# Sparse attention feeding a token mixer: the values of a pair of query blocks in two halves, by batch

## The chip, the cores and the metric

The kernel runs on one core of one Trainium2 chip. The metric is the device time of one execution in microseconds (us), lower is better. TensorE is PE in the profile, VectorE is DVE, ScalarE is ACT, GpSimd is POOL and SyncE, which issues most DMAs, is SP.

## The reference, cut to what matters

Four batches, eight heads, 768 positions in 24 blocks of 32, head size 64. Every query block attends to the first and the last block, to its neighbours and to three sampled blocks; the first and the last query block attend to all. The result goes through a mixing layer.

```python
scores = scale * np.matmul(q, k.transpose(0, 1, 3, 2))
mask = np.abs(blk_i - blk_j) <= window            # window = 1, blocks of 32
mask = mask | (blk_i == 0) | (blk_j == 0) | (blk_i == n_blocks - 1) | (blk_j == n_blocks - 1)
for qb in range(n_blocks):
    for kb in sampled_blocks[qb]:
        mask[qb * block:(qb + 1) * block, kb * block:(kb + 1) * block] = True
attn = softmax(np.where(mask, scores, -1e9))
x = np.matmul(attn, v)                            # heads side by side: [4, 768, 512]
theta = x @ w_theta
y = w_tok_r @ (x * cos(theta)) + w_tok_i @ (x * sin(theta))     # over positions, by batch
u = x + y
out = u + np.maximum(u @ w_ch, 0.0)
```

## The kernel before

The program has two parts, `attention` (until about 265 us) and `token_mix` (the rest). Attention goes through the batches in two passes of two batches each, `bp` 0 and 1; in the code below `b` is the batch within the pass. A pass is a row of **units**: four wide units for the first and the last query block (names with `w`), then 22 narrow units, one for each query block `i` from 1 to 22. Two neighbouring narrow units, `i` odd and `i + 1`, make a **pair**, and what the program does from one odd unit to the next is called a **step** here. The order of all instructions is written out by hand (`tc.manual_schedule()`); each engine runs its own list in order.

A narrow block goes through these stages, with the names of their tiles:

- `gather_k` (POOL): copies the block's keys into `kg`: five copies for an odd block, four for an even one. `gather_v` (POOL): an indirect DMA that fetches the block's value rows into one of four buffers `vb`. `load_pair` (SP): a plain load of the values that the two blocks of a pair share, into `va`.
- `scores` (PE): sixteen matmuls into PSUM tile `S` (two buffers); then two reductions on DVE to `m` (the row minima).
- `weights` (ACT): four exponentials from `S` to `P`.
- `turn` (PE, ACT): eight transposes of `P` into the PSUM tile `T`, of which there is one, two banks wide; a copy on ACT from `T` to `pT`. `pT` holds both blocks of a pair, and there is one `pT`.
- `values` (PE): for a whole pair, into the PSUM tile `X` (one, a bank for each batch): for each batch one matmul that zeroes the bank, sixteen small matmuls with `vb` and eight with `va`; here for both batches at once.
- `finish` (DVE, SP): three DVE instructions (`sm`, `sm`, `xo`) and four stores of `xo` to the scratch `xs` in DRAM.

Between these, `Decoder` turns the 64-bit weights of the mixer into float32 pieces: `load` (SP, 512 KB), `start` (ACT, an Abs), `bits` (DVE, three instructions), `rest` (two), `high` (ACT, a cast), `low` (two), in which the next but one piece is loaded. `decoder.ahead(phases)` puts the ACT part at the head of a unit, `decoder.go(phases)` the DVE part behind the weights.

In the step of before, an odd unit `i` has on PE: scores of `i + 1`, values of the pair `i - 2`, transposes of `i`. The even unit behind it has scores of `i + 2` and transposes of `i + 1`. On ACT the odd unit has weights before the copy, the even unit the copy before the weights; so two copies stand behind each other, with at most a decoder instruction between.

Both parts overlap at the end of attention: `follow` is the generator of `token_mix`, and its pieces (`theta`, whose products are the PSUM tiles `h`, and then ACT's `t`, the first reader of `h`) are put between the last units by `next(follow)`.

Of the kernel before, what the change touches and what calls it, by code (L numbers as in the profile page):

```python
# [10 lines left out]
F32 = mybir.dt.float32  # L11
# [9 lines left out]
P = 128  # L21
# [165 lines left out]
def attention(tc, qT, qE, kT, vr, sampled, xs, ident, pieces, room, follow):  # L187
# [8 lines left out]
    nc = tc.nc  # L196
    with ExitStack() as ctx, ExitStack() as scored, ExitStack() as early:
# [10 lines left out]
        ps_t = ctx.enter_context(tc.tile_pool(name="ps_t", bufs=1, space=PSUM))  # L208
# [6 lines left out]
        none = first[0:1, 1:2].bitcast(BF16)[:, 0:1]  # L215
# [7 lines left out]
        kbs, qbs, qes, vws, st, xws, numbers = {}, {}, {}, {}, {}, {}, {}  # L223
# [97 lines left out]
        def turned(pts, out, name):  # L321

            t = ps_t.tile([P, 8, 128], F32, tag="T", name=f"T{name}")
            for k, pt in enumerate(pts):
                nc.tensor.transpose(t[:, k, :], pt, ident)  # L325
            t = t[:, 0 : len(pts)]
            nc.scalar.copy(out, t.rearrange("r k (p q) -> r k p q", p=4) if len(out.shape) == 4 else t)  # L327

        pT_pair = pT.rearrange("r (k p u q) -> r k p u q", k=8, p=4, u=2)
        pT_wide = pT.rearrange("r (e k f) -> r e k f", e=2, k=8)  # L330

        def turn(bp, i):
            s = st[bp, i]
            pts = [s["P"][:, e, b, 128 * c : 128 * c + 128] for c in range(2) for e in range(2) for b in range(2)]
            turned(pts, pT_pair[:, :, :, (i - 1) % 2, :], f"{bp}_{i}")

        def normalised(name, x, n):
            sm = wp.tile([P, 8], F32, tag="sm", name=f"sm{name}", bufs=2)[:, 0:n]
# [8 lines left out]
        def sums_tile(name):  # L347
            return ps_x.tile([P, 2, 512], F32, tag="X", name=f"X{name}")[:, :, 0:260].rearrange("r b (g f) -> r b g f", f=65)

        def values(bp, i):
            x = st[bp, i]["X"] = sums_tile(f"{bp}_{i}")
            va = vas[((i - 1) // 2) % VA_BUFS]
            def weigh(b, e, p, k, u0, n, v, start, stop):
                c, pp = p // 2, p % 2
                r0 = 64 * c + 32 * u0
                v0 = 65 * (8 * b + 4 * pp + 2 * e + c)
                nc.tensor.matmul(  # L359
                    x[r0 : r0 + 32 * n, b, 2 * pp + e, :], pT_pair[:, 4 * k + 2 * e + b, p, u0 : u0 + n, :], v[:, v0 : v0 + 65],  # L360
                    start=start, stop=stop,
                )

            heads = [(b, e, p) for b in range(2) for e in range(2) for p in range(4)]
            for b in range(2):
                nc.tensor.matmul(x[:, b], none.to_broadcast([1, P]), none.unsqueeze(2).to_broadcast([1, 4, 65]), start=True, stop=False)
            for b, e, p in heads:
                for u in range(2):
                    weigh(b, e, p, 1, u, 1, vbs[(i - 1 + u) % VB_BUFS], False, False)
            for b, e, p in heads:  # L370
                weigh(b, e, p, 0, 0, 2, va, False, e == 1 and p % 2 == 1)

        def finish(bp, i):
            xo = normalised(f"{bp}_{i}", st.pop((bp, i))["X"], 8)
            for c in range(2):
                for u in range(2):
                    r0 = 64 * c + 32 * u
                    nc.sync.dma_start(xs[bp][i + u, c].rearrange("q b p f -> q (b p f)"), xo[r0 : r0 + 32])
# [64 lines left out]
        units = []  # L443
# [8 lines left out]
        def do(n, inner, wide=None):  # L452

            if 0 <= n < len(units):
                bp, i, x = units[n]
                if i != "w":
                    inner(bp, i)
                elif wide:
                    wide(bp, *x)

        def is_wide(n):
            return 0 <= n < len(units) and units[n][1] == "w"
# [6 lines left out]
        with tc.manual_schedule():  # L469
            load_edges(0)  # L470
            load_k(0, 0, 2)
            tab = Tables(nc, wp, sampled)
            turn_edges(0)
            load_k(0, 2, 2)
            load_v_wide(0, 0, 0)
            load_k(0, 4, 2)
            load_v_wide(0, 0, 1)
            load_k(0, 6, 2)
            load_v_wide(0, 1, 0)
            load_v_wide(0, 1, 1)  # L480
            for i in (1, 3):
                load_q(0, i)
            decoder = Decoder(pieces, stage, nc.sync)
            do(0, scores, scores_wide)
            tab.make(nc, cp)
            do(0, weights, weights_wide)
            for n in range(len(units) + 1):
                phases = 0
                if n < len(units):
                    phases = round(shares[n] / total * 3 * len(pieces)) - decoder.at  # L490
                if n + 5 < len(units) and not is_wide(n + 5) and units[n + 5][:2] not in ((0, 1), (0, 3)):
                    load_q(*units[n + 5][:2])
                if first_of_pair(n + 10):
                    load_edges(1)
                if first_of_pair(n + 12):
                    load_v_wide(1, 0, 0)
                if first_of_pair(n + 2):
                    for b, pp in WIDE[1:]:
                        load_v_wide(1, b, pp)
                do(n + 2, gather_k)  # L500
                if n == len(units) - 5:
                    follow.send(qp)
                elif n == len(units) - 3:
                    next(follow)
                if 5 <= n < 21 and n % 2:
                    load_k(1, (n - 5) // 2, 1)
                do(n + 3, number_blocks)
                do(n + 2, scale_q)
                if first_of_pair(n + 2):
                    turn_edges(1)  # L510
                decoder.ahead(phases)
                last = None
                if is_wide(n):
                    bp, _, x = units[n]
                    if n and not is_wide(n - 1):
                        last = units[n - 2][:2]
                        values(*last)
                    turn_wide(bp, *x, 0)
                    do(n + 1, scores, scores_wide)
                    if n and is_wide(n - 1):  # L520
                        values_wide(bp, *units[n - 1][2], 1)
                    if is_wide(n + 1):
                        nx = units[n + 1]
                        weights_wide(nx[0], *nx[2], (0,))
                        turn_wide(bp, *x, 1)
                        weights_wide(nx[0], *nx[2], (1,))
                    else:
                        do(n + 1, weights, weights_wide)
                        turn_wide(bp, *x, 1)
                    if last:  # L530
                        finish(*last)
                    decoder.go(phases)
                    if n == 0:
                        tab.rest(nc)
                    values_wide(bp, *x, 0)
                    if n and is_wide(n - 1):
                        finish_wide(bp, *units[n - 1][2])
                elif n == len(units):
                    last = units[n - 2][:2]
                    values(*last)  # L540
                    next(follow)
                    finish(*last)
                else:
                    bp, i, _ = units[n]
                    do(n + 1, scores, scores_wide)
                    if i == 1:
                        values_wide(bp, *units[n - 1][2], 1)
                    elif i % 2:
                        last = bp, i - 2
                        values(*last)  # L550
                    if n == len(units) - 1:
                        scored.close()
                        next(follow)
                    if i % 2:
                        do(n + 1, weights, weights_wide)
                        turn(bp, i)
                    else:
                        turn(bp, i)
                        do(n + 1, weights, weights_wide)
                    decoder.go(phases)  # L560
                    if last:
                        finish(*last)
                    if n >= len(units) - 2:
                        if n == len(units) - 2:
                            early.close()
                        next(follow)
                    if i == 1:
                        finish_wide(bp, *units[n - 1][2])
                do(n + 2, load_pair)
                do(n + 2, gather_v)  # L570
            assert not decoder.left(), decoder.left()


# [298 lines left out]
```

## Time and profile before

| | us |
|---|---|
| three runs | 607.76, 609.36, 615.38 |
| median | 609.36 |
| the profiled execution | 603.66 |
| its span | 601.9 |

The profiled execution is 5.70 us under the median of the runs. Its page has PE busy for 545.9 us (91% of the span), DVE 444.2 (74%), ACT 346.1 (58%) and POOL 150.3 (25%). The granted clock of PE is 0.971 in the mean. In the profile's answers a row has a start, a duration, the engine, the source line, the operation, the tiles written and read, a count, and in brackets the idle time ahead of it with what ended it; "issue" is an end for which the profile shows no cause. A matmul on float32 data of which the program has one stands as two in the counts (S, X).

### The profile page before, as it was taken

Reading aid. Unit: us, or ns where it says so; the run is one execution under the profiler, and the core shown is the slowest. Engines: PE = TensorE matmul, PEld = TensorE weight load, DVE = VectorE, ACT = ScalarE, POOL = GpSimd, SP = SyncE. Lnnn points to the kernel's source line nnn. Section 1 sums busy time; section 2 is a strip of 40 time slices with the busy share of each in tenths; the row PEclk is TensorE's granted clock in tenths of the full one; section 3 lists DMA queues with packets and bytes.
Section 4 is the critical chain, followed back from the end, with each engine's and each line's share of the span. In section 5 each row is a group of like instructions: output and inputs, shape, how many; then the busy total and the mean of one; then the engine's idle time right before and its main releaser. Section 6 shows DMA issues by size and latency. Waiting matters only on the chain.

```text
span 601.9 us, 16838 instructions
## 1 busy us (share of the span) xinstructions
PE 545.9 (91%) x6636; PEld 481.1 (80%) x6636; DVE 444.2 (74%) x1041; ACT 346.1 (58%) x730; POOL 150.3 (25%) x262
## 2 busy tenths in 40 slices
PE   4878787897798988489999999999999999999997
PEld 2556555565565666479999999999999999999997
DVE  3799768878998998598974985757857649548454
ACT  2667757866688787755664743455634456424520
POOL 1459758640578795000000000000000000000000
PEclk9989979998999999959999999999999999999999
DMA  8879999995689899455221241211431111221002
GB/s 296 325 219 313 330 277 354 305 316 174 204 252 285 286 319 256 141 158 143 86 71 35 75 145 57 75 43 50 119 107 62 61 49 32 77 69 60 16 1 105
DMA packets 63263, 95.60 MB, mean 159 GB/s; under 512 B 9168, under 2 KB 44624, under 8 KB 63184
## 3 DMA queue, kind: packets, MB, share of 16 engines
q1 hardware_dynamic: 56848, 71.09, 38.6%
q0 software_dynamic: 6336, 23.43, 11.5%
q8 instruction: 52, 0.85, 0.6%
q14 instruction: 27, 0.22, 0.1%
HBM read 81.90 MB, written 12.58 MB: 157 GB/s over the span
## 4 chain that ended last, share of the span: by engine, by line
PE 76%; DVE 9%; ACT 7%; issue 4%; DMA 3%; SPq 1%; ACTq 0%; DVEq 0%
PE y L676 11%; PE y L677 11%; PE y L678 11%; PE T L325 6%; PE X L359 6%; PE S L307 4%; PE o L701 4%; PE o L700 4%; PE o L699 4%; PE h L638 4%; PE h L640 4%; PE h L639 4%; ACT pT L327 3%; ACT P L319 2%; DMA raw_tok_r<-in_w_tok_r_dram 2%
## 5 line engine op out<-in xcount | busy, mean ns | idle before, releaser
L319 ACT ACTIVATE P<-S,m 128x256 f32<-128x256 f32 x176 | 69.3, 485 | 15.4 <-DVE m L310 12.2
L642 ACT ACTIVATE t<-h,up_int 128x256 f32<-128x256 f32 x48 | 22.8, 475 | 74.5 <-PE h L640 74.2
L310 DVE TENSOR_REDUCE m<-S 128x2 f32<-128x512 f32 x88 | 56.3, 681 | 12.4 <-PE S L307 12.4
L307 PE MATMUL S<-kg,q 64*32 64x256 f32 x1408 | 54.9, 402 | 8.3 <-issue 8.3
L638 PE MATMUL h<-w_theta_hi,xTh 128*128 128x256 f32 x192 | 55.8, 291 | 6.9 <-ACT xTh L629 6.8
L327 ACT COPY pT<-T 128x1024 f32<-128x1024 f32 x44 | 44.8, 1019 | 30.0 <-PE T L325 29.7
L325 PE MATMUL T<-ident,P 128*128 128x128 f32 x352 | 49.1, 283 | 14.0 <-ACT pT L327 11.4
L325 PEld LDWEIGHTS T<-ident,P 128*128 128x128 f32 x352 | 38.4, 143 | 27.3 <-ACT pT L327 21.3
L268 POOL COPY kg<-kb 128x256 f32 (+2 forms) x101 | 53.0, 565 | 19.8 <-PE S L307 19.7
L640 PE MATMUL h<-w_theta_hi,xTl 128*128 128x256 f32 x192 | 55.5, 289 | 1.6 <-DVE xTl L630 1.6
L268 POOL COPY kg<-kb_tok_i 128x256 f32 (+2 forms) x101 | 50.8, 542 | 24.2 <-DVE sb_scratch L175 14.8
L639 PE MATMUL h<-w_theta_lo,xTh 128*128 128x256 f32 x192 | 55.2, 287 | 0.0
L290 POOL DMA_INDIRECT vb<-in_vr_dram,rows x44 | 44.5, 1012 | 39.6 <-PE X L359 33.5
L645 DVE SCALAR_TENSOR_TENSOR rr<-t,h 128x256 f32<-128x256 f32 x48 | 19.8, 414 | 34.6 <-ACT t L643 34.1
L649 ACT ACTIVATE cs<-rr 128x256 f32<-128x256 f32 x48 | 20.0, 416 | 43.5 <-DVE rr L647 43.5
L638 PEld LDWEIGHTS h<-w_theta_hi,xTh 128*128 128x128 f32 x192 | 37.4, 195 | 7.9 <-ACT xTh L629 7.9
L677 PE MATMUL y<-w_tok_r,zh 128*128 128x384 f32 x128 | 43.1, 337 | 0.0
L677 PE MATMUL y<-w_tok_i,zh 128*128 128x384 f32 x128 | 43.1, 337 | 0.0
L678 PE MATMUL y<-w_tok_i,zl 128*128 128x384 f32 x128 | 43.1, 337 | 0.0
L676 PE MATMUL y<-w_tok_i,zh 128*128 128x384 f32 x128 | 43.1, 337 | 0.0
L678 PE MATMUL y<-w_tok_r,zl 128*128 128x384 f32 x128 | 43.1, 337 | 0.0
L676 PE MATMUL y<-w_tok_r,zh 128*128 128x384 f32 x128 | 43.1, 336 | 0.0
(154 smaller groups left out, 1467.7 us busy)
## 6 DMA issues: line engine op xcount, KB each, us to landing
xa<-xs SPq DMA_DIRECT2D x192, 64.0 KB
xr<-xs SPq DMA_DIRECT2D x96, 64.0 KB
out_dram<-of SPq DMA_DIRECT2D x32, 192.0 KB
va<-in_vr_dram SPq DMA_DIRECT2D x22, 260.0 KB
q<-in_qT_dram SPq DMA_DIRECT2D x22, 256.0 KB
xs<-xo SPq DMA_DIRECT2D x88, 64.0 KB
raw_tok_r<-in_w_tok_r_dram SPq DMA_DIRECT2D x9, 512.0 KB
raw_tok_i<-in_w_tok_i_dram SPq DMA_DIRECT2D x9, 512.0 KB
```

Of the source, the lines that this page charges most:

```text
L268: nc.gpsimd.tensor_copy(dst, blocks.rearrange("r g s f -> r s g f"))
L307: nc.tensor.matmul(sc[32 * p : 32 * p + 32, e, b, :], q[rows, b, p, :], keys[rows, :, :, place(b, p), :], start=True, stop=True)
L310: nc.vector.tensor_reduce(m[:, e], sc[:, e], axis=AX.X, op=ALU.min)
L319: nc.scalar.activation(pt[:, e, b, :], sc[:, e, b, :], AF.Exp, bias=m[:, e, b : b + 1], scale=-1.0)
L325: nc.tensor.transpose(t[:, k, :], pt, ident)
L327: nc.scalar.copy(out, t.rearrange("r k (p q) -> r k p q", p=4) if len(out.shape) == 4 else t)
L638: nc.tensor.matmul(ps, hi[:, c, :], wh[:, c, :], start=c == 0, stop=False)
L639: nc.tensor.matmul(ps, hi[:, c, :], wl[:, c, :], start=False, stop=False)
L640: nc.tensor.matmul(ps, lo[:, c, :], wh[:, c, :], start=False, stop=c == 3)
L676: nc.tensor.matmul(acc, zh[:, dd], wh[j][:, tt], start=j == 0 and m == 0, stop=False)
L677: nc.tensor.matmul(acc, zh[:, dd], wl[j][:, tt], start=False, stop=False)
L678: nc.tensor.matmul(acc, zl[:, dd], wh[j][:, tt], start=False, stop=j == 5 and m == 1)
```

## The change

The values of a pair are split by batch. Batch 0 of the pair is done in the even unit, right behind the second transposition of that pair; batch 1 in the next step, where both stood before. The transposes are sorted by batch, so that each of the two banks of `T` holds one batch, and each bank has its own copy to `pT`, 512 columns wide instead of one copy of 1024. `finish` now stands ahead of `decoder.go`, and the two value gathers of a pair are issued together in the odd unit.

```diff
         def turn(bp, i):
-            s = st[bp, i]
-            pts = [s["P"][:, e, b, 128 * c : 128 * c + 128] for c in range(2) for e in range(2) for b in range(2)]
-            turned(pts, pT_pair[:, :, :, (i - 1) % 2, :], f"{bp}_{i}")
+            pt, u = st[bp, i]["P"], (i - 1) % 2
+            t = ps_t.tile([P, 8, 128], F32, tag="T", name=f"T{bp}_{i}")
+            for b in range(2):
+                for k in range(4):
+                    c, e = k // 2, k % 2
+                    nc.tensor.transpose(t[:, 4 * b + k, :], pt[:, e, b, 128 * c : 128 * c + 128], ident)
+                nc.scalar.copy(pT_pair[:, b:8:2, :, u, :], t[:, 4 * b : 4 * b + 4].rearrange("r k (p q) -> r k p q", p=4))
...
-        def values(bp, i):
-            x = st[bp, i]["X"] = sums_tile(f"{bp}_{i}")
+        def values(bp, i, b):
+            if not b:
+                st[bp, i]["X"] = sums_tile(f"{bp}_{i}")
+            x = st[bp, i]["X"]
...
-            heads = [(b, e, p) for b in range(2) for e in range(2) for p in range(4)]
-            for b in range(2):
-                nc.tensor.matmul(x[:, b], none.to_broadcast([1, P]), none.unsqueeze(2).to_broadcast([1, 4, 65]), start=True, stop=False)
+            heads = [(b, e, p) for e in range(2) for p in range(4)]
+            nc.tensor.matmul(x[:, b], none.to_broadcast([1, P]), none.unsqueeze(2).to_broadcast([1, 4, 65]), start=True, stop=False)
...
                     elif i % 2:
                         last = bp, i - 2
-                        values(*last)
+                        values(*last, 1)
...
                         turn(bp, i)
                         do(n + 1, weights, weights_wide)
-                    decoder.go(phases)
+                        values(bp, i - 1, 0)
                     if last:
                         finish(*last)
+                    decoder.go(phases)
...
                 do(n + 2, load_pair)
-                do(n + 2, gather_v)
+                if is_wide(n) or is_wide(n + 2):
+                    do(n + 2, gather_v)
+                elif n < len(units) and units[n][1] % 2:
+                    do(n + 2, gather_v)
+                    do(n + 3, gather_v)
```

The two other calls of `values` (behind the last pair of a pass) become `values(*last, 1)` as well.

How it moves the instructions is shown at three places. The first is PE's list in the second pass, from the transposes of block 9 on; `T1_9` is the tile T of pass 1 and block 9, and X is named after the pair's first block. Before:

```order
L325 MATMUL T1_9_3416<-ident_58,P1_9_3315 128x128 x8
L307 MATMUL S1_11_3457<-kg_120,q1_11_3103 32x256 x16
L325 MATMUL T1_10_3477<-ident_58,P1_10_3411 128x128 x8
L307 MATMUL S1_12_3512<-kg_120,q1_11_3103 32x256 x16
L366 MATMUL X1_9_3532<-first_117 128x260
```

After, without the sixteen rows with `vb` ahead of each row with `va`:

```order
L338 MATMUL T1_9_3446<-ident_58,P1_9_3346 128x128 x8
L307 MATMUL S1_11_3489<-kg_120,q1_11_3131 32x256 x16
L338 MATMUL T1_10_3509<-ident_58,P1_10_3441 128x128 x8
L371 MATMUL X1_9_3525<-first_117 128x260
...
L365 MATMUL X1_9_3525<-va0_122,pT_121 64x65 x8
L307 MATMUL S1_12_3570<-kg_120,q1_11_3131 32x256 x16
L371 MATMUL X1_9_3525<-first_117 128x260
...
L365 MATMUL X1_9_3525<-va0_122,pT_121 64x65 x8
L338 MATMUL T1_11_3620<-ident_58,P1_11_3520 128x128 x8
```

The first half of X moved from behind the scores of block 12 to ahead of them; there, the matmul ahead of it is the transposition whose copy it reads.

The second place is the end of attention on PE, where theta's first products `h0` stand behind the last transposition, T1_22. Before:

```order
L325 MATMUL T1_22_4497<-ident_58,P1_22_4414 128x128 x8
L638 MATMUL h0_4507<-w_theta_hi_75,xTh0_0_4473 128x256
L639 MATMUL h0_4507<-w_theta_lo_76,xTh0_0_4473 128x256
...
L366 MATMUL X1_21_4555<-first_117 128x260
```

After:

```order
L338 MATMUL T1_22_4540<-ident_58,P1_22_4456 128x128 x8
L371 MATMUL X1_21_4551<-first_117 128x260
...
L365 MATMUL X1_21_4551<-va0_122,pT_121 64x65 x8
L648 MATMUL h0_4577<-w_theta_hi_75,xTh0_0_4516 128x256
L649 MATMUL h0_4577<-w_theta_lo_76,xTh0_0_4516 128x256
```

Half of the last pair's values moved ahead of theta. ACT's list there is the same in both kernels: two casts to `xTh`, the load of a function table, `early`, then the copy of T1_22, then `t`.

The third place is SP's list at the end of the first pass, with the loads of the mixer's weights (`raw`), of the wide units' values (`vw`) and the stores of `xo`. Before:

```order
L391 DMA vw1_tok_i_2163<-in_vr_dram 128x6x260 x3
L61 DMA raw_tok_r_2048_2259<-in_w_tok_r_dram 128x1024
L378 DMA xs0_73<-xo0_19_2267 32x512 x4
```

After:

```order
L396 DMA vw1_tok_i_2209<-in_vr_dram 128x6x260 x3
L383 DMA xs0_73<-xo0_19_2281 32x512 x4
L61 DMA raw_tok_r_2048_2289<-in_w_tok_r_dram 128x1024
```

The load of a piece of weights moved behind the four stores of the pair before; the same happens in the other odd units whose `decoder.go` ends a piece.

More of the change, by code (lines that the diff above doesn't have):

```diff
@@ L326, in turned @@
             t = t[:, 0 : len(pts)]
-            nc.scalar.copy(out, t.rearrange("r k (p q) -> r k p q", p=4) if len(out.shape) == 4 else t)
+            nc.scalar.copy(out, t)
         pT_pair = pT.rearrange("r (k p u q) -> r k p u q", k=8, p=4, u=2)
@@ L539, in attention @@
                     last = units[n - 2][:2]
-                    values(*last)
+                    values(*last, 1)
                     next(follow)
@@ L549, in attention @@
                         last = bp, i - 2
-                        values(*last)
+                        values(*last, 1)
                     if n == len(units) - 1:
```

## The prediction

> **What bounds the kernel now.** I cut the span into stages first; here are the narrow blocks of both passes (from 44 and from 166 us) and the mixer. Columns: the stretch, its length, busy time and count of PE, PE's weight loads, DVE, ACT and POOL, then PE's clock, the share of the DMA engines, GB/s.
>
> ```profile
> 44.00:129.50 85.50, 72.83 (x1734) 50.50 (x1734) 70.97 (x127) 62.12 (x124) 60.83 (x100) 0.95 0.99 311
> 166.00:236.50 70.50, 63.05 (x1611) 44.60 (x1602) 63.65 (x116) 57.30 (x114) 59.01 (x94) 0.99 0.92 281
> 265.00:601.90 336.90, 332.71 (x2063) 332.36 (x2062) 229.69 (x615) 160.45 (x380) 0.00 (x0) 0.99 0.24 71
> ```
>
> The mixer fills PE (332.71 of 336.90 us), and the change leaves it alone: what attention gains or loses arrives at the end unshortened. In the narrow stages no engine is full. PE has 85% and 89%, DVE 83% and 90%, and the DMA engines are taken for 99% of the first stage. So I looked for what PE waits for, and for how short a step can be.
>
> ```profile
> PE T L325 <- ACT pT L327: 11.4, 7, 2.9
> DVE m L310 <- PE S L307: 12.4, 11, 4.5
> PE S L307 <- issue: 8.3, 6, 3.0
> ACT pT L327 <- PE T L325: 29.7, 30, 5.8
> ```
>
> Seven long waits of the transposes for ACT's copy make 11.4 us. DVE waits for scores as long as that, and PE has 8.3 us inside scores that no engine explains, up to 3.0 us at a time. ACT, on its part, waited for T ahead of 30 of its 44 copies. The shortest step is this one:
>
> ```profile
> 221.35 0.40 PE L366 MATMUL X<-first 1*128 1x260 bf16 x2
> ...
> 223.88 1.10 PE L325 MATMUL T<-ident,P 128*128 128x128 f32 x8
> 224.90 1.09 PE L307 MATMUL S<-kg,q 64*32 64x256 f32 x32
> 226.13 1.09 PE L325 MATMUL T<-ident,P 128*128 128x128 f32 x8
> 227.16 1.09 PE L307 MATMUL S<-kg,q 64*32 64x256 f32 x32
> 228.18 0.40 PE L366 MATMUL X<-first 1*128 1x260 bf16 x2
> ```
>
> From X to X it is 228.18 - 221.35 = 6.83 us: X 2.53, T 1.02, S with a gap 1.23, T 1.03, S 1.02. The gap of 0.2 us ahead of the second T is the copy that has not quite ended. Everything else is PE's own work, which the change keeps (the same matmuls, in another order). Long waits look like this:
>
> ```profile
> 215.39 1.27 DVE L310 TENSOR_REDUCE m<-S 128x2 f32<-128x512 f32 x2
> 216.78 1.57 ACT L319 ACTIVATE P<-S,m 128x256 f32<-128x256 f32 x4 [1.14 <-DVE m L310]
> 218.22 1.03 ACT L327 COPY pT<-T 128x1024 f32<-128x1024 f32 x1
> 219.30 0.87 PE L325 MATMUL T<-ident,P 128*128 128x128 f32 x6 [1.66 <-ACT pT L327]
> ```
>
> DVE's reduction was late, behind the decoder; the exponentials wait for it, the copy for them on ACT, and T for the copy. So the copy is the last link of a chain that DVE starts.
>
> **Step 1, the copy in halves.** Its price comes from two sizes of the same copy, from the exponentials' row in the page, and from the copy behind the T of 223.88.
>
> ```profile
> L327 ACT COPY pT<-T x44: 995/1012/1119, 39.5 to 246.1; 128x1024 f32<-128x1024 f32 x44
> L327 ACT COPY pT<-Tw x16: 778/798/816, 12.1 to 156.7; 128x768 f32<-128x768 f32 x16
> L319 ACT ACTIVATE P<-S,m 128x256 f32<-128x256 f32 x176 | 69.3, 485 | 15.4 <-DVE m L310 12.2
> ...
> 225.06 1.01 ACT L327 COPY pT<-T 128x1024 f32<-128x1024 f32 x1
> ```
>
> 256 columns less save 0.214 us, so 512 should take 0.585, about 0.60. Four exponentials of 0.485 take 1.57 above, not 1.94: neighbours overlap by about 0.1, and two half copies take 1.1 us against 1.01. ACT does 0.09 us more in each of 44 units, 4 us in all, which I cost at nothing: ACT is idle for 23 of 85.50 and 13 of 70.50 us. Without that cover it is the 4 us.
>
> The next T needs only the first bank, 0.41 us sooner than the whole copy: seven long waits lose 7 x 0.41 = 2.9 us, and the 0.2 us gap goes in the other fifteen pairs: 3.0 us. **Minus 5.9 us**; between none and all of the waits, 11.4 + 3.0 = 14.4.
>
> **Step 2, the first half of X behind its own transposition.** It reads a copy that has just become possible. Four transposes end about 0.63 us after T's start (0.28 + 3 x 0.115, since eight take 1.09), ACT follows 0.08 later (223.88 + 1.10 = 224.98, and the copy is at 225.06), the copy takes 0.60, and PE 0.05: X may start 1.36 us after T. PE is there after 1.03 + 0.20 (the zeroing, half of 0.40): it waits 0.13. In 16 of 22 even units ACT has a decoder instruction between the two copies; where it is ready, the wait is about 0.2. In three (blocks 7, 17 of the first pass, 9 of the second) it is a cast of what DVE makes in the unit before, now behind `finish`:
>
> ```profile
> 127.85 0.16 DVE L340 TENSOR_SCALAR sm<-X 128x8 f32<-128x8 f32 x1
> 128.04 0.20 DVE L341 RECIPROCAL sm<-sm 128x8 f32<-128x8 f32 x1
> 128.28 0.69 DVE L344 TENSOR_TENSOR xo<-X,sm 128x512 f32<-128x512 f32 x1
> ...
> 212.27 0.52 DVE L70 TENSOR_SCALAR da_tok_i<-da_tok_i 128x512 f32<-128x512 f32 x1
> 212.82 0.50 DVE L71 TENSOR_SCALAR da_tok_i<-da_tok_i 128x512 int32<-128x512 int32 x1
> 213.35 0.77 DVE L72 SCALAR_TENSOR_TENSOR da_tok_i<-raw_tok_i,da_tok_i 128x512 int32<-128x512 int32 x1
> 215.00 0.64 ACT L86 CAST w_tok_i<-da_tok_i 128x512 fp32r<-128x512 f32 x1
> ```
>
> From the end of scores: reduction 1.38, `finish` 1.04, `bits` 1.8, cast 0.64, copy 0.60: 5.5 us. PE comes after half X 1.27, T 1.03, S 1.02, T 1.03, zeroing 0.20: 4.55. It waits 0.95. So 3 x 0.95 + 13 x 0.2 + 6 x 0.13 = **plus 6.3 us**. Bounds: nothing, where DVE sets the pace anyway; and 0.95 in all 22 units, 20.9 us. Behind the waiting X stand the next scores, and behind them DVE. I take the middle reckoning, nearest to the rows of an undisturbed step.
>
> **Step 3, queues that are passed.** POOL issues both gathers behind the second half of X instead of one; the keys for the scores two further on come about 1.1 us later, and those scores stand 1.3 us later, behind half an X: nothing, with the same narrow margin. `finish` ahead of the decoder delays decoder pieces by 1.04 us and their loads on SP by the four stores. One place pays, where the first pass ends:
>
> ```profile
> 126.47 9.57 DMA raw_tok_r<-in_w_tok_r_dram
> ...
> 129.00 1.76 SPq L378 DMA_DIRECT2D xs<-xo  x4
> ```
>
> The wide stage starts when this load lands, 9.57 us after its issue. Now `finish` (1.04) is ahead of it on DVE and four stores (1.76) on SP; `low`, two DVE instructions, runs beside the stores: **plus 1.0 us**, between nothing (if the bytes queued ahead set the landing) and 1.2.
>
> **Step 4, the hand-over to the mixer.** Here the first half of X goes ahead of theta.
>
> ```profile
> 241.91 1.09 PE L325 MATMUL T<-ident,P 128*128 128x128 f32 x8 [1.16 <-ACT pT L327]
> 243.87 0.28 PE L639 MATMUL h<-w_theta_lo,xTh 128*128 128x256 f32 x1
> 243.99 0.28 PE L640 MATMUL h<-w_theta_hi,xTl 128*128 128x256 f32 x1
> 246.12 1.00 ACT L327 COPY pT<-T 128x1024 f32<-128x1024 f32 x1
> 247.02 0.48 ACT L642 ACTIVATE t<-h,up_int 128x256 f32<-128x256 f32 x1
> 258.07 0.41 PE L640 MATMUL h<-w_theta_hi,xTl 128*128 128x256 f32 x1
> 258.28 0.41 PE L638 MATMUL h<-w_theta_hi,xTh 128*128 128x256 f32 x1
> 265.08 0.66 PE L676 MATMUL y<-w_tok_r_hi,zh 128*128 128x384 f32 x1
> ```
>
> T ends at 243.0, but ACT reaches its copy at 246.12 (a table load stands ahead). Before, theta filled that time; now X waits until 246.12 + 0.60 + 0.05 = 246.77, and theta's first twelve products come behind it. At full speed (0.12 us apart) h is ready after 1.27 + 1.57 at 249.6, and `t` starts 2.6 us later than at 247.02. But PE has then idled for 3.8 us, and a gap of 3.0 us at 73.84 shows what follows:
>
> ```profile
> 74.00:77.00 3.00, 0.13 (x8) 0.79 1.03 352
> 78.00:80.00 2.00, 2.00 (x16) 0.50 1.01 268
> ```
>
> The clock falls to 0.50. Products 0.21 us apart, as at 258, and half an X of 1.6 give 251.1: `t` 4.1 us later. The chain of what ended last runs through `t`, DVE and two more loads to the mixer's first y at 265.08 with no slack shown, so I take **plus 4.0 us**, between 2.6 and 4.1.
>
> The Trainium skill, "TensorE: Matmul & The Clock Gate", section "Part 1: The HAM clock gate (the "warmup" mystery)", speaks against this part of the change: PE falls to half clock after an idle window of about 3.4 us, and the window runs freely, so that 3.8 us of idling need not hold a whole one. By that alone the term lies anywhere from 2.6 to 4.1; the trace's drop after 3.0 us is earlier than the rule, and I go by the row.
>
> **The sum.** -5.9 + 6.3 + 1.0 + 4.0 = +5.4 us: 609.1 by the profiled execution (603.66). That execution lies 5.7 us under the median of the runs; on the median, 609.36 + 5.4 = **614.8 us**, 0.9% slower. About 2% (12.2 us) is what a measurement of this kernel can tell from no change.
>
> **Rivals.**
> - *The pace evens out* (faster). From one S to the next PE now works 1.27 + 1.03 + 1.02 = 3.3 and 1.03 + 0.13 + 1.27 + 1.02 = 3.5 us, where it was 4.6 and 2.25. DVE has a reduction (1.28) and a decoder share in each unit and `finish` in every other one, which fits even spacing better; its 12.4 us of waiting for scores speak for this. Then steps are DVE's, X's waits cost nothing and all 14.4 us of waits go: -14.4 + 5.0 = -9.4, 600 us. Against it: the first stage has its DMA engines full, and PE's gaps within scores stay. Chance 0.27, of it 0.12 beyond 2% (with part of DVE's waiting too, under 597).
> - *X waits for ACT in every step* (slower). If 0.95 us is the rule, not the exception: 20.9 - 5.9 + 5.0 = +20, 629 us. It decides from a mean wait of 0.6 us: 22 x 0.6 - 5.9 + 5.0 = 12.3. For it: ACT is in order and has an extra instruction in 16 of 22 units. Against it: the 30 of 44 copies where ACT was there first. Chance 0.15.
> - *The banks don't separate.* If T waits for both halves, the -5.9 falls away and the copy is 0.09 longer in 22 pairs: 614.8 + 5.9 + 2.0 = 622.7, just over 2%. Chance 0.1.
>
> **How the numbers follow.** The forecast has 0.48. Under 597 lies 0.12; the slow rival and half of the third one are over 2%: 0.2; so 0.68 within. The range from 600 to 627 holds the forecast with its bounds, the third rival and the milder half of the fast one.
>
> **What would show it.** Step 1: T's waits for pT under 7 us. Step 2: a wait of X's `vb` matmuls for pT of 0.1 to 0.3 us in most even units, and copies near 600 ns. Step 3: the load at the end of the first pass behind the stores, the wide stage 1 us later. Step 4: PE idle for nearly 4 us behind T1_22 and the first y 4 us later against the last narrow step. I am wrong if X's waits lie where DVE sets the pace, or if gathers issued in twos lengthen PE's unexplained gaps.

## The result, and the profile after

| | before | after |
|---|---|---|
| median of the runs (us) | 610.69 (607.76 to 615.38, 4 runs) | 650.13 (649.56 to 651.0, 4 runs) |
| ratio, 95% interval | | 1.064 [1.057, 1.071] |
| the profiled execution, its span | 603.66, 601.9 | 650.02, 648.2 |
| mean granted clock of PE | 0.971 | 0.962 |

The kernel became 6.4% slower; 614.8 us was forecast, and the range ended at 627. A ratio here leaves out runs of a kernel that lie over 1.5% above its fastest one; executions of the kernel before spread from 602 to 622 us over all comparisons, so a ratio within 1% of it says little, as an unchanged copy will show.

The groups of the page after that answer to those of before. Behind the bar are busy time and mean ns of one, then the engine's idle time ahead of them and what ended it:

```profile
L338 PE MATMUL T<-ident,P 128*128 128x128 f32 x352 | 60.9, 298 | 60.3 <-ACT pT L339 60.3
...
L310 DVE TENSOR_REDUCE m<-S 128x2 f32<-128x512 f32 x88 | 56.5, 684 | 47.9 <-PE S L307 47.6
...
L339 ACT COPY pT<-T 128x512 f32<-128x512 f32 x88 | 52.0, 590 | 50.9 <-PE T L338 50.9
...
L307 PE MATMUL S<-kg,q 64*32 64x256 f32 x1408 | 50.0, 394 | 0.0
```

The transposes now wait 60.3 us for ACT's copy, where they waited 11.4. The copy itself waits 50.9 us for the transposes (29.7 before), and DVE 47.6 us for scores (12.4). PE waits for ACT, and ACT and DVE wait for PE, each far longer than before, which is what a serial chain looks like. At the same time PE's 8.3 us of idle time within scores that no engine explained are gone. The waits of PE for ACT show how the 60.3 us are spread, in total, times, and longest:

```profile
PE T L338 <- ACT pT L339: 60.3, 45, 5.6
```

45 waits for 44 narrow units: it is every unit, not some. By the trace each unit has one of them between its fourth and its fifth transposition, 59.6 of the 60.3 us; the one left over, 0.73 us, stands ahead of a unit. A stretch of the second pass shows one even unit (the first group of T, at 264.02) and one odd unit (at 270.01) on PE and ACT:

```profile
264.02 0.66 PE L338 MATMUL T<-ident,P 128*128 128x128 f32 x4
...
264.77 0.59 ACT L339 COPY pT<-T 128x512 f32<-128x512 f32 x1
...
265.41 0.66 PE L338 MATMUL T<-ident,P 128*128 128x128 f32 x4 [0.73 <-ACT pT L339]
266.00 0.28 PE L371 MATMUL X<-first 1*128 1x260 bf16 x1
266.16 0.59 ACT L339 COPY pT<-T 128x512 f32<-128x512 f32 x1 [0.80 <-PE T L338]
266.21 0.69 PE L365 MATMUL X<-vb,pT 128*32 128x65 f32 x32
...
268.52 0.28 PE L371 MATMUL X<-first 1*128 1x260 bf16 x1
...
270.01 0.66 PE L338 MATMUL T<-ident,P 128*128 128x128 f32 x4
270.10 1.57 ACT L319 ACTIVATE P<-S,m 128x256 f32<-128x256 f32 x4 [1.36 <-PE X L365]
...
271.54 0.60 ACT L339 COPY pT<-T 128x512 f32<-128x512 f32 x1
...
272.20 0.65 PE L338 MATMUL T<-ident,P 128*128 128x128 f32 x4 [1.53 <-ACT pT L339]
```

Eight transposes no longer stand together. The first four end, the copy of *their* half runs, and only when it has ended do the second four start, 0.06 us later. In the even unit that costs the copy and its start, 0.73 us. In the odd unit ACT has the four exponentials of the next unit ahead of the copy, and PE waits 1.53 us. X's first half, which I had expected to wait, finds its copy long done.

The program says the same. In PE's list of the kernel after, here for block 12 of the first pass, a row that waits for another engine says so; the fifth transposition of a unit has a wait on ACT of its own, for the count that the copy of the first half raises:

```
L338 MATMUL T_12_1485<-ident,P_12_1417 128x128 [waits Activation_49]
L338 MATMUL T_12_1485<-ident,P_12_1417 128x128 x3
L338 MATMUL T_12_1485<-ident,P_12_1417 128x128 [waits Activation_49]
L338 MATMUL T_12_1485<-ident,P_12_1417 128x128 x3
```

Both halves write one tile `T`, and the program orders the second write behind the read of the first half that stands ahead of it in the list, though that read is of another bank. The stages, between the starts of the first and last rows of S, of the wide scores and of y, in us of the profiled executions:

| | before | after |
|---|---|---|
| first narrow S to the wide stage of pass 2 | 96.5 | 112.8 |
| wide stage of pass 2 | 26.4 | 26.3 |
| first to last S of pass 2 | 83.7 | 109.2 |
| last S to first y | 28.8 | 36.1 |
| first y to the end | 336.8 | 334.1 |

The loss sits in the narrow stages and in the hand-over. Its parts: T's waits 60.3 - 11.4 = +48.9. X costs more as well: from its zeroing to the next group a half takes 270.01 - 268.52 = 1.49 us, against 223.88 - 221.35 = 2.53 for both halves before, so 22 x (2 x 1.49 - 2.53) = +9.9. And PE's unexplained idle time from 40 us to the end of attention, 14.5 us before, is gone: -14.5. That makes 44.3 of the 46.3 us between the two spans, but the sum is not complete: the page's busy time of the transposes grew too, from 49.1 to 60.9 us (four alone take 0.66 us, eight together 1.10), and that of the scores fell from 54.9 to 50.0 us.

### The profile page after: what moved, and what is told of

It is laid out like the page before. It is cut to its first block, busy times and chain, and to the rows that moved or that the text cites. A ratio compares the mean times of both kernels' runs of the same rounds, so it can differ in the third digit from the quotient of the medians.

```text
span 648.2 us, 16861 instructions
## 1 busy us (share of the span) xinstructions
PE 560.2 (86%) x6636; PEld 485.8 (75%) x6636; DVE 450.7 (70%) x1041; ACT 352.4 (54%) x774; POOL 136.4 (21%) x262
## 2 busy tenths in 40 slices
DMA packets 63263, 95.60 MB, mean 147 GB/s; under 512 B 9168, under 2 KB 44624, under 8 KB 63184
## 3 DMA queue, kind: packets, MB, share of 16 engines
q1 hardware_dynamic: 56848, 71.09, 35.9%
q0 software_dynamic: 6336, 23.43, 11.4%
## 4 chain that ended last, share of the span: by engine, by line
PE 78%; ACT 10%; DVE 6%; DMA 3%; issue 2%; SPq 1%; ACTq 0%; DVEq 0%
PE y L686 10%; PE y L688 10%; PE y L687 10%; PE X L365 9%; PE T L338 6%; PE S L307 6%; ACT P L319 5%; ACT pT L339 4%; PE h L650 3%; PE o L709 3%; PE o L711 3%; PE o L710 3%; PE h L648 3%; PE h L649 3%; PE SW L406 2%
## 5 line engine op out<-in xcount | busy, mean ns | idle before, releaser
L338 PE MATMUL T<-ident,P 128*128 128x128 f32 x352 | 60.9, 298 | 60.3 <-ACT pT L339 60.3
L310 DVE TENSOR_REDUCE m<-S 128x2 f32<-128x512 f32 x88 | 56.5, 684 | 47.9 <-PE S L307 47.6
L339 ACT COPY pT<-T 128x512 f32<-128x512 f32 x88 | 52.0, 590 | 50.9 <-PE T L338 50.9
L290 POOL DMA_INDIRECT vb<-in_vr_dram,rows x44 | 42.4, 963 | 80.7 <-PE X L365 72.4
L268 POOL COPY kg<-kb 128x256 f32 (+2 forms) x101 | 45.7, 495 | 30.0 <-PE S L307 29.9
L268 POOL COPY kg<-kb_tok_i 128x256 f32 (+2 forms) x101 | 46.5, 502 | 25.6 <-DVE sb_scratch L174 15.0
L307 PE MATMUL S<-kg,q 64*32 64x256 f32 x1408 | 50.0, 394 | 0.0
L710 PE MATMUL o<-ul,w_ch_hi 128*128 128x384 f32 x128 | 42.9, 335 | 0.0
```

Source lines behind the costliest of these rows:

```text
L268: nc.gpsimd.tensor_copy(dst, blocks.rearrange("r g s f -> r s g f"))
L307: nc.tensor.matmul(sc[32 * p : 32 * p + 32, e, b, :], q[rows, b, p, :], keys[rows, :, :, place(b, p), :], start=True, stop=True)
L338: nc.tensor.transpose(t[:, 4 * b + k, :], pt[:, e, b, 128 * c : 128 * c + 128], ident)
L339: nc.scalar.copy(pT_pair[:, b:8:2, :, u, :], t[:, 4 * b : 4 * b + 4].rearrange("r k (p q) -> r k p q", p=4))
L710: nc.tensor.matmul(ps, wh[:, c, :], ul, start=False, stop=False)
```

## The experiments

Medians are in us, with the span of the runs. Beside them the kernel before had 611.3 (runs 1 to 4), 611.2 (5 to 8), 611.0 (9 to 12) and 609.1 (13 and 14).

### 1 to 4. Which part holds the loss

First, T in two tiles of one bank (the six transposes of a wide unit stand in them as four and two; `T_9h` in the rows is both tiles of block 9):

```diff
-            t = ps_t.tile([P, 8, 128], F32, tag="T", name=f"T{bp}_{i}")
             for b in range(2):
+                t = ps_t.tile([P, 4, 128], F32, tag=f"T{b}", name=f"T{bp}_{i}h{b}")
...
```

> The kernel after with one edit: T is two tiles of one bank each, one for each batch, instead of one tile of two banks; every other order stays. Theory A (the second four transposes of a unit wait for the copy of the first four, because both halves lie in one tile): T's waits for pT inside a unit go; of the 60.3 us of PE idle ahead of T at most 12 stay, the 9.79 us steps fall below 8.6, and the time is 605 to 622 us. Theory B (the values in halves wait for ACT, or their split costs too much): 640 us or more, since the values stay in halves. Theory C (passed queues, the order of finish and of the gathers): 640 or more as well.

Measured: 623.2 (618.6 to 626.0), 1.020 [1.011, 1.029]. 27 of the 39 us came back by this edit alone. The rows of an odd unit (9) and an even one (10) in the second pass:

```profile
201.51 1.09 PE L339 MATMUL T_9h<-ident,P 128*128 128x128 f32 x8
202.53 1.09 PE L307 MATMUL S<-kg,q 64*32 64x256 f32 x32
203.70 1.15 PE L339 MATMUL T_10h<-ident,P 128*128 128x128 f32 x8
204.78 0.28 PE L372 MATMUL X<-first 1*128 1x260 bf16 x1
204.99 0.30 PE L366 MATMUL X<-vb,pT 128*32 128x65 f32 x2
205.65 0.68 PE L366 MATMUL X<-vb,pT 128*32 128x65 f32 x30 [0.35 <-ACT pT L340]
```

All eight stand together again, and now X's first half waits where I had placed its wait, by 0.35 us. T's waits for pT sum to 14.9 us (the groups of before had 11.4), where at most 12 had been expected, and the time is 1 us over the top of Theory A's span: 12 us of the loss are not the tile's.

Second, one tile, but the order changed so that no copy stands between the transposes:

```diff
             for b in range(2):
                 for k in range(4):
                     ...
-                nc.scalar.copy(pT_pair[:, b:8:2, :, u, :], ...)
+            for b in range(2):
+                nc.scalar.copy(pT_pair[:, b:8:2, :, u, :], ...)
```

> The kernel after with one edit: the eight transposes of a unit stand together, and the two half copies behind them; T stays one tile. Theory A: no wait within T is left, though the next T waits for both copies: 612 to 630 us, up to 10 us more than with two tiles, and the 0.73 and 1.4 us waits in the middle of T are gone from the trace. Theory B or C: 640 or more.

Measured: 633.4 (632.2 to 636.5), a miss by 3 us, on the slow side. The waits within T are gone, but the next T needs both copies:

```profile
PE T L338 <- ACT pT L340: 22.1, 19, 3.2
```

Third, the turn of the kernel after in the kernel before, the values whole:

```diff
-            turned(pts, pT_pair[:, :, :, (i - 1) % 2, :], f"{bp}_{i}")
+            for b in range(2):
+                for k in range(4):
+                    ...
+                nc.scalar.copy(pT_pair[:, b:8:2, :, u, :], ...)
```

> The kernel before with one edit: the transposes by batch and the two half copies of the kernel after, in one tile; the values stay whole in the next step, finish and gathers as before. Theory A: the waits within T alone bring most of the loss: 22 x (0.73 + 1.4) = 47 us less what they hide of before's 11.4: 635 to 655 us. Theory B or C: within 2% of before (597 to 622).

Measured: 648.3 (645.7 to 649.0). These lines alone, with nothing moved elsewhere, bring 37 of the 39 us:

```profile
PE T L338 <- ACT pT L339: 45.2, 44, 3.9
```

Fourth, the reverse: the whole copy of before, all else as after.

> The kernel after with one edit: the transposes and the one copy of 1024 columns of the kernel before; the values stay in halves, finish and gathers as after. Theory A: no wait within T, but the first half of X waits for the whole copy, about 1.0 + 0.1 - 0.2 = 0.9 us in each of 22 pairs, 20 us, and 5 to 10 us for the split: 618 to 640 us. Theory B: 645 or more, as slow as after or slower.

Measured: 638.3 (637.5 to 639.6). X's first half waits for a whole copy in every pair, 21.2 us where 20 had been reckoned, and T for as much:

```profile
PE X L361 <- ACT pT L327: 21.2, 22, 3.7
PE T L325 <- ACT pT L327: 21.0, 19, 2.9
```

The four agree on the main cause: the two kernels in which the second four transposes stand behind the copy of the first four, in one tile, lose 37 and 39 us, without and with values in halves. The three without that order still lose 12, 22 and 27 us; the last two have other waits for a copy instead, those shown for the next T and for X.

### 5, 6, 8 and 9. The rest of the change, with T in two tiles

Parts are set back to the order of before. The hand-over first:

```diff
                     last = units[n - 2][:2]
+                    values(*last, 0)
                     values(*last, 1)
...
-                        values(bp, i - 1, 0)
+                        if n < len(units) - 1:
+                            values(bp, i - 1, 0)
```

> The kernel with two one-bank tiles T (623.2 us, 2.0% over before), and the first half of the last pair's X set back behind theta's first products; all other pairs stay in halves. What is left of the loss has two candidates. Theory D (the hand-over): X's first half waits 3.71 us for the copy behind the table load, theta comes behind it, and the first y follows the last scores after 35.9 us against 28.8 before: the time falls by 4 to 7 us, to 616 to 619. Theory E (the hand-over is hidden elsewhere; all of the loss lies in the pairs): 621 to 625, no change.

Measured: 616.6 (613.6 to 620.9), 6.7 us less. Theory D. The place in the run with two tiles, where the hand-over is as in the kernel after; then the granted clock of the idle time, of the 5 us behind it, and of the next 4 (length, busy PE, PEld, DVE, ACT and POOL, clock, DMA share, GB/s):

```profile
258.89 0.30 PE L366 MATMUL X<-vb,pT 128*32 128x65 f32 x2
262.90 1.11 PE L366 MATMUL X<-vb,pT 128*32 128x65 f32 x30 [3.71 <-ACT pT L340]
263.93 1.19 PE L366 MATMUL X<-va,pT 128*64 128x65 f32 x16
265.05 0.58 PE L649 MATMUL h<-w_theta_hi,xTh 128*128 128x256 f32 x1
```
```profile
259.20:262.90 3.70, 0.00 (x1) 0.00 (x1) 1.66 (x6) 2.63 (x5) 0.00 (x0) 0.85 0.51 141
262.90:268.00 5.10, 5.10 (x60) 4.81 (x61) 0.00 (x0) 0.43 (x1) 0.00 (x0) 0.50 0.39 98
268.00:272.00 4.00, 3.23 (x61) 2.74 (x60) 1.14 (x3) 2.58 (x7) 0.00 (x0) 0.92 0.02 4
```

PE idles 3.71 us for the copy, then runs at half clock for 5 us. With X set back, the first y follows the last scores after 27.9 us, not 35.9.

All three parts set back, the two below with the hand-over:

> As the run with the hand-over set back, and also finish behind the decoder and each gather of values by itself, as in the kernel before: what stays of the change is the values in halves and T in two tiles. Theory F (the split costs, 22 x (2 x 1.49 - 2.53) = 9.9 us of PE, and passed queues cost nothing): the same time as the run with only the hand-over set back, within 3 us. Theory G (passed queues: DVE's decoder behind finish, gathers in twos): 5 us or more below it, 605 to 612.

Measured: 611.3 (608.0 to 613.6), 1.000 [0.997, 1.004] of the kernel before, in Theory G's span. The gathers alone:

```diff
-                if is_wide(n) or is_wide(n + 2):
-                    do(n + 2, gather_v)
-                elif n < len(units) and units[n][1] % 2:
-                    do(n + 2, gather_v)
-                    do(n + 3, gather_v)
+                do(n + 2, gather_v)
```

> The kernel with two one-bank tiles T and each gather of values by itself again, one behind each unit; all else as after. Theory F: 621 to 625 us, no change. Theory G for the gathers: 4 us or more below 623.

Measured: 620.5 (617.9 to 625.6), 2.7 us less, between the spans of both theories and with ranges that overlap: not told from nothing. And `finish` alone:

```diff
-                    if last:
-                        finish(*last)
                     decoder.go(phases)
+                    if last:
+                        finish(*last)
```

> The kernel with two one-bank tiles T, and finish behind the decoder's share again as in the kernel before; gathers in twos and the hand-over as after. With all three set back the time was 611.3, with the hand-over alone 616.6, with the gathers alone 620.5, against 623.2. Theory G for finish (DVE's decoder share behind finish makes the reductions and ACT's casts late): 617 to 621 us. Theory F (the order of finish costs nothing, the 5 us are the gathers'): 622 to 625.

Measured: 617.3 (615.6 to 623.8), in the span of Theory G. By the medians the order of `finish` cost 5.9 us, though one of the four runs lies among those of the kernel with two tiles. T's waits for pT fall from 14.9 to 4.0 us: with `finish` behind, they are those at the two starts of the narrow stages and at T_22. With the hand-over that makes 623.2 - 6.7 - 5.9 = 610.6, against 611.3 for all three, so nothing that can be told is left for the gathers. And nothing is left for the split of X, although its 9.9 us of PE are still done. That needed a reason.

### 7 and 10. Where a gain goes: PE runs out of instructions

The kernel before, values whole, with T in two tiles and two copies:

```diff
-            turned(pts, pT_pair[:, :, :, (i - 1) % 2, :], f"{bp}_{i}")
+            for b in range(2):
+                t = ps_t.tile([P, 4, 128], F32, tag=f"T{b}", name=f"T{bp}_{i}h{b}")
+                for k in range(4):
+                    ...
+                nc.scalar.copy(pT_pair[:, b:8:2, :, u, :], ...)
```

> The kernel before with T in two one-bank tiles, transposes by batch and two half copies; the values whole in the next step, all else as before. Theory A (the fault was the one tile, the halves of the copy are good): the 11.4 us of T's waits fall to about half, and the time is 600 to 607 us against 609 to 611. Theory H (the copy is not what sets the pace of before, DVE's chain is): within 2 us of before.

Measured: 611.1 (602.4 to 616.5), ratio 0.993 [0.988, 0.998]; and the kernel before, unchanged, against itself:

> The kernel before, unchanged, for a second profile of it, since its first one lay 6 us under the median of its runs. Theory I (PE runs out of instructions where it is quick: the idle time without a shown cause ends when a packet of 16 KB on the instruction queue has landed, late under full DMA engines): the gaps stand at other places, 12 to 22 us in sum, each ending 1.2 to 1.6 us behind the landing of such a packet. Theory J (the gaps belong to certain instructions): the same places as in the first profile.

Measured: 608.9 (602.3 to 616.2), 0.993 [0.988, 0.998]. The same ratio, so the two tiles brought nothing that can be told: Theory A misses, and the time alone would speak for Theory H. T's waits did not fall much, 8.8 us where the two profiles of before have 11.4 and 14.3; but PE's idle time without an engine to blame grew. Its rows, in the kernel with two tiles:

```profile
PE X L364 <- issue: 15.6, 9, 3.2
...
PE S L307 <- issue: 3.5, 4, 1.5
...
PE T_5h L339 <- issue: 2.0, 1, 2.0
```

21.1 us, against 14.5 before (8.3, 4.8 and 1.4) and 14.0 in its second profile. (The profiled execution with two tiles took 615.0 us, 4 us over the median, so a part of its gaps may be its own.) One of these gaps, and the DMA queues in the two stretches into which the landing of one packet divides it (share of 16 engines last):

```profile
95.62 1.15 PE L364 MATMUL X<-va,pT 128*64 128x65 f32 x29
99.97 0.33 PE L364 MATMUL X<-va,pT 128*64 128x65 f32 x3 [3.21 <-issue]
```
```profile
q1 hardware_dynamic: 139, 0.33, 94.3%
q0 software_dynamic: 8, 0.03, 12.5%
q8 instruction: 1, 0.02, 6.1%
```
```profile
q0 software_dynamic: 58, 0.24, 54.0%
q1 hardware_dynamic: 95, 0.20, 44.2%
```

The first stretch is 97.40 to 98.50: a packet of 16 KB on the instruction queue starts at 97.41, when PE already stands still, and lands at 98.47; the second, 98.50 to 99.97, has none. PE goes on 1.50 us behind the landing, in the middle of a group of equal matmuls. This holds for all gaps of 0.2 us and more between 40 and 265 us: 13 of 13 in the first profile of before (1.26 to 1.68 us behind a landing), 9 of 10 in the second, 14 of 14 here. The gaps stand at other instructions each time, as Theory I had it. The page has the queue's sum:

```profile
q8 instruction: 52, 0.85, 0.6%
```

PE executes 6636 matmuls and 6636 weight loads, 13,272 instructions. If the queue's 0.85 MB are theirs, that is 64 bytes each, and a packet holds 256 of them; 52 x 256 = 13,312 fits. A narrow step has about 356 of them and takes 7 to 8 us, so by this estimate a packet lasts PE some 5 to 6 us, and it is fetched while the DMA engines are taken for 92% to 99% of the time.

The Trainium skill, "Runtime: NRT & Kernel Launch", section "Instruction fetch mechanics", describes it: instruction memory is a queue that the sequencer refills in blocks of 16 KiB by DMA of its own, and the cost of crossing from one block to the next is "mostly hidden". The trace agrees on the blocks (52 packets, 0.85 MB) and differs on the hiding: 14.5 us of PE's time are not hidden here.

### 11 to 14. The same kernels with fewer bytes in the air

Most pieces of the mixer's weights are loaded to an eighth; the instructions stay, and the mixer computes with wrong weights.

```diff
-        queue.dma_start(self.raw, self.src.rearrange("p (f w) -> p f w", w=2))
...
+            self.raw, n = of.raw, self.f // 8
+            queue.dma_start(self.raw[:, 0:n], src[:, 0:n])
...
```

> The kernel before with an eighth of the decoder's loads: from the third piece on, only 64 of the 512 columns of a weight piece are loaded, so the weights of the mixer are wrong and 10 x 448 KB of DMA traffic during attention are left out; every instruction stays. Theory I: with the DMA engines freer the instruction packets land in time, PE's 14.5 us of gaps without a cause fall under 5, the wide stage starts earlier, and the time is 592 to 603 us. Theory J: gaps of 10 us or more stay, over 605.

> The kernel before with T in two one-bank tiles and two half copies (values whole), and an eighth of the decoder's loads as in the run beside it. With full loads T's waits for pT had fallen but PE's gaps without a cause had grown from 14.5 to 21.1 us, and the time had stayed. Theory I (the gain of the halves went into waiting for instructions): the gaps fall under 6 us, and the kernel is now 3 to 8 us faster than the kernel before with the same thin loads. Theory H (the copy never set the pace): within 2 us of it.

Measured: 602.1 (600.5 to 602.9) and 596.6 (594.0 to 601.1). The page's sum of DMA traffic falls from 95.60 to 86.42 MB, so it was 20 pieces that became thin, not the 10 of the expectation. PE's gaps without a cause, in the kernel before with thin loads:

```profile
PE S L312 <- issue: 1.5, 2, 1.2
PE T L330 <- issue: 1.2, 2, 0.8
PE X L364 <- issue: 0.8, 2, 0.5
```

14.5 fell to 3.5 us, and 9 us of time went with it, near the 11 us of the gaps (loads that are waited for got shorter too, which this run does not separate). With two tiles 21.1 fell to 7.7, over the 6 expected, and two tiles are now 5.4 us faster than one, which Theory H does not allow. The last pair repeats the run with two tiles and asks for the split of X:

> The kernel with T in two one-bank tiles and the values in halves (hand-over, finish and gathers as before), with an eighth of the decoder's loads. Theory K (the halves' extra PE work of 9.9 us only fills gaps in which PE would have waited for instructions): without the gaps it shows, and this is 4 to 10 us slower than whole values with thin loads (596.6): 601 to 607. Theory L (the even pace gains as much as the split costs): within 3 us of it, 594 to 600.

> The partner of the run beside it, with whole values, as measured before at 596.6 us (593.98 to 601.07): 594 to 600 again. Against the kernel before with thin loads (602.1) Theory I expects 3 us or more less.

Measured: 597.6 (595.8 to 599.7) with whole values and 602.4 (601.8 to 604.5) in halves. The runs of the two do not overlap. Theory K, at its lower end: the split costs 4.8 us when PE waits less for instructions, and nothing when it waits for them anyway. In this repeat PE's gaps with whole values are 11.4 us, in halves 3.1, so the thin loads took away half of them with whole values, not all, and the 4.8 us need not be all that the split costs. The rows of PE, whole and then in halves, show the trade:

```profile
PE X L369 <- issue: 7.7, 5, 2.6
...
PE S L312 <- issue: 3.7, 3, 1.6
```
```profile
PE X L377 <- DVE xo L354: 3.6, 7, 0.9
PE S L312 <- issue: 2.1, 4, 0.8
...
PE X L371 <- ACT pT L345: 1.7, 5, 0.5
```

The split saves 8.3 us of gaps (11.4 to 3.1) and 2.0 us of T's waits for pT; it pays 9.9 us of work, and 5.6 us of waits of X for the copy and for DVE's `finish` of the pair before. That makes +5.2, where the spans differ by 4.8.

So the split itself takes gaps away, with full loads too. The kernel with all three parts set back and the one with two tiles and whole values differ in the split alone and take the same time, 611.3 and 611.1 us; in place of 21.1 us the first has 7.1:

```profile
PE X L366 <- issue: 4.2, 5, 1.4
...
PE S L307 <- issue: 2.9, 3, 1.4
```

Over all profiles with full loads the gaps between 40 and 265 us are 12.4 to 21.1 us in the four with whole values and 0 to 8.4 in the eight with values in halves.

No version here beats the kernel before with its full loads; the best, T in two tiles with whole values, equals it.

## Why the prediction was wrong, step by step

- **What bounds the kernel** was read by half. "PE has 8.3 us inside scores that no engine explains" was in the quoted rows and then left out of the sum. It is PE waiting for instructions, and the place into which a gain of PE can disappear.
- **Step 1 failed**, where it says "The next T needs only the first bank" and books a gain for it. The size of the copy was right (590 ns against 585 to 600), but the term had the wrong sign. I asked what the next T's first half waits for, and not what the second half of the *same* T stands behind: the copy of the first half, in the same tile, and in odd units four exponentials too. Minus 5.9 was put down; the run that adds only this brings +37 us, and the one that takes only it away -27. With the banks really apart about the -5.9 appears with thin loads: -5.4 in runs made together, -4.5 to the repeat. With full ones it can't be seen, and the longer gaps for instructions say where it went.
- **Step 2** put +6.3 on X's waits. In the kernel after they are nothing, since T's wait hides them. With two tiles they are 6.3 us in six waits, but 3.71 of these are the hand-over, so about 2.5 in the narrow steps: over-sized. Left out was that the same matmuls cost more in two groups than in one, 0.45 us a pair for X; "the same matmuls, in another order" was taken as free.
- **Step 3** had nothing for the gathers, which held as far as can be told, and +1.0 for `finish`, at the load ahead of the wide stage. That stage took 26.3 us against 26.4, so the place was wrong; yet `finish` ahead of the decoder costs about 5.9, by the traces through copies that come late for T (14.9 against 4.0 us of waits).
- **Step 4** had the mechanism: 3.8 us of idling were reckoned and, with two tiles, 3.71 measured, with the half clock behind them (0.50) and products 0.21 us apart. (In the kernel after it is the second half of T1_22 that waits there, 4.15 us.) With two tiles `t` stood 268.08 - 253.6 = 14.5 us behind the last scores where it stood 247.02 - 236.3 = 10.7 before, 3.8 later against 4.1 reckoned. Only the size of the term was short, 6.7 against 4.0, since the first y comes 7.1 us later, not 3.8; behind `t`, X's second half and the stores and loads of xs that follow it are on the chain that ended last too.
- **Rivals.** The third had the right suspicion at 0.10, that the banks do not separate, and a wrong price: it let T wait at its start for both halves, 0.09 us longer in 22 pairs and without the gain of step 1, 7.9 us in all, in place of twice four transposes with a copy between. At 0.73 in 22 even and 1.34 to 1.53 us in 22 odd units it would have given 46 to 50 us. Of the first, the even pace did come (the starts of S stand 4.49 and 5.29 us apart in turn through most of the kernel after, where 2.25 and 4.6 to 6 were common), but evenly slow: a step takes 9.78 us. The second, X waiting in every step, is what the whole copy brings (22 waits, 21.2 us), not the half ones.

## What to carry to other kernels

Before halving a copy to let an engine start earlier, look up at which grain the program orders writes and reads: here both halves were one tile, and a copy written between two groups of writes made the second group wait for it; a tile for each half avoided that, and both copies behind the writes did so at the price of a longer wait at the next unit. Price a split also on the engine that does the same work in more groups. And idle time without a cause is part of the bound: here it was instruction supply under full DMA engines, and it seems to swallow what PE gains elsewhere.

## What the runs showed of the hardware that was not expected

PE stops in the middle of a run of equal matmuls, by up to 3.2 us, when its next 16 KB of instructions come late; it goes on 1.2 to 1.7 us after they have landed (36 of 37 gaps in three profiles). Without 9.2 of the 95.6 MB of DMA traffic the gaps of the kernel before fell from 14.5 to 3.5 us. A kernel does not lose them by being slow: the one with the new turn alone, at 648 us, keeps 12.4 us of them, while the kernel after, at 650 us and with X in halves, has none between 40 us and the end of attention.

A group of small matmuls costs more in parts. The 24 for one batch of X with their zeroing take 1.49 us by themselves, those of both batches in one go 2.53.

The granted clock falls sooner behind a stop of PE than the prediction took it to. It went from 1.00 to 0.50 at 1.9 us into the gap of 3.0 us in the kernel before (at 75.72), 2.6 us into the hand-over's gap with two tiles (261.79), and 0.7 us into that of the kernel after (284.73).
